# Gate logits of the first 512 tokens on VectorE, and a new order of all tasks

## The chip, the cores and the metric

The kernel runs on one core of a Trainium2 chip. Times are device microseconds (us) of one execution. Smaller is better. TensorE (PE) multiplies matrices into PSUM, VectorE (DVE), ScalarE (ACT) and GpSimd (POOL) work on tiles, and SyncE (SP) issues every DMA of this kernel.

## The reference

Two branches over 2,048 tokens with 512 features are mixed by a gate of one number per token.

```
x = A_x                                            # 2048 x 512
g = sigmoid(sum(x * gate_w, -1))                   # one gate per token
# A: attention, 32 heads of 16, causal, a window of 256 tokens
q, k, v = split_heads(x @ wqkv)
s = q @ k.T * 16 ** -0.5;  s = where(0 <= i - j < 256, s, -1e9)
a = join_heads(softmax(s) @ v) @ wo
# B: a layernorm over features, then an MLP over tokens
h = (x - mean) / sqrt(var + 1e-5)
u = gelu(h.T @ w1 + b1)                            # 512 x 1376
b = (u @ w2 + b2).T
out = g * a + (1 - g) * b
```

## The kernel before

All of x stays in SBUF (`xo`), with its transpose by blocks of 512 tokens (`XT`). The first block is transposed on PE, the other three by DMA (`xt1` to `xt3`).

The work is cut into some 1,100 named tasks, each of which runs on one engine and issues a few instructions:

- `q`, `k`, `v`: projections (chains of matmuls over 128 features each; line 670 is the helper `chain` that issues all full matmuls). `qc`, `kc`, `vc` copy their results from PSUM. The copy of the queries always runs on DVE (line 754).
- `s3.v1` and the like: scores of 128 queries of a visit (here visit 3) against 128 keys for sixteen heads, row-tiled on PE (line 942); `sj.C` are the corners of the window (line 1042); `ej...` is the exponential on ACT (line 894), `mj...` the mask, on DVE (lines 907, 974) or on POOL (line 536).
- `pv3.0` and the like: probabilities times values, column-tiled on PE (line 1087). Then `n1` to `n4` on DVE: a transpose out of PSUM (line 1178), the reciprocal of the row sums, their product with the gate's factor, and the transpose back into `xo`.
- `bs`, `ba`, `pow`, `h`: layernorm on DVE and POOL. `u0` to `u10`: the first MLP product (16 matmuls each), `ub` its bias, `gelu` in one task on ACT. `y0` to `y15`: 11 matmuls of the second MLP product and 4 of the output projection in one accumulation; `f` scales and adds the bias, `o` stores.
- The gate. For the first block (`NGP = 1`), `gate0` multiplies the transposed block with gate_w on PE (16 matmuls with one column, line 802), and `gatem0` takes the result out of PSUM. For the other blocks, `gl4` to `gl15` on DVE multiply and add up along the features (line 822), from a copy of gate_w on all partitions which the load `gw` brings. `gatee` (ACT) takes the exponential, `ez` (DVE) spreads it for `nz`.

Nothing in the kernel decides its order while it runs. `PLAN` is a written list of tasks for each engine, with the PSUM bank or buffer of each task after a colon (`s3.v1:64`). The function `arrange` (line 85) plays the lists through with costs per task, which gives the one order in which instructions are issued; each engine then works through its own list in order. The costs in `arrange` do not reach the chip, except in one respect: the order in which tasks of different engines are issued, and with it a wait that POOL gets when a two-input DVE task is near.

PE's tasks have a mode: full array (d), row-tiled scores (s), corners (c), column-tiled products (p, and h for the corners' own). The chunks of projections and MLP products may run full or column-tiled. The set `THEN` names the scores and products after which the full chunks that follow run column-tiled, that is, with four matmuls of 32 rows of output in place of one.

SP's list sets the order of loads. Before: `x0`, `wqk0` to `wqk3`, `x1.4`, the transposed load `xt1`, `wv`, `x2.8`, `bias`, `xt3`, `x3.12`, `xt2`, then w1; `gw` comes among the w1 loads. A task at the head of the list that waits holds all loads behind it. w2 lies in the memory of w1, so its loads wait for the MLP's first product.

Of the kernel before, what the change touches and what calls it, by code (L numbers as in the profile page):

```python
# [78 lines left out]
SWITCH = 0.095  # L79

BLOCK, AHEAD, FETCH, BUSY = 256, 80, 3.6, 3.0
LATENCY = {"PE": 0.22, "ACT": 0.15, "DVE": 0.12, "POOL": 0.15, "SP": 2.0}


def arrange(tasks):
# [21 lines left out]
    while len(order) < len(tasks):  # L107
# [19 lines left out]
        t.cost = t.engines[e]  # L127
        ins = t.ins
        if e == "PE":
            new = then if t.flex else t.mode  # L130
            if new != mode:
                t.cost += SWITCH
            if t.flex and new == "p":
                t.tiled = True
                ins *= 4
            if t.mode != "d":
                then = "p" if t.name in THEN else "d"
            mode = new
# [52 lines left out]
        warm:3 xta0.0.0:7 xta0.0.1:6 warmb xta0.1.1:4 xta0.1.0:5 q1_0.0:2 k3_0.0:3 k1_0.0:6 q3_0.0:1 k0_0.0:7  # L191
        q3_0.1 q0_0.0:0 k3_0.1 q1_0.1 q1_0.2 k1_0.1 k3_0.2 k0_0.1 q0_0.1 q2_0.0:5 q1_0.3 q0_0.2 q1_0.4 q0_0.3
        k3_0.3 q3_0.2 q0_0.4 k3_0.4 q3_0.3 k2_0.0:4 q2_0.1 k0_0.2 k1_0.2 k1_0.3 k0_0.3 k1_0.4 q2_0.2 q3_0.4 q2_0.3
        k0_0.4 k2_0.1 k2_0.2 k2_0.3 k2_0.4 q2_0.4 s0.v0:62 q3_1.0:0 q3_1.2 k3_1.0:1 k3_1.2 q0_1.0:7 s0.C:42 v1.0:6
        q0_1.2 s-1.C:02 v1.2 v2.0:5 v2.2 s1.v3:02 biast:4 v0.0:7 v0.2 v3.0:5 v3.2 q1_1.0:4 s1.v0:62 v5.0:1 q1_1.2
        gate0:5 v5.2 v14.0:0 s0.v1:62 v13.0:5 k2_1.0:1 v14.2 pv-1.0:6 v10.0:4 k2_1.2 v13.2 s1.v2:26 k2_2.0:0 v10.2
        v15.0:1 v12.0:5 v12.2 v15.2 k2_2.2 pv0.0:2 pv0.1 s1.v1:64 pv0.2 v4.0:1 v4.2 k3_2.0:0 k3_2.2 s2.v1:26 v7.0:5
        v7.2 k0_2.0:4 s1.C:60 k0_2.2 v6.0:3 v6.2 s2.v3:06 k0_1.0:2 k0_1.2 k1_1.0:5 k1_1.2 pv1.0:6 pv1.1 pv1.2
        s2.v0:02 v11.0:4 v11.2 v8.0:5 v8.2 pv1.3 pv1.4 s2.v2:20 q2_1.0:5 v9.0:4 q2_1.2 s2.C:26 v9.2 k1_2.0:1 k1_2.2
        u3.0:0 u3.2 s3.v1:64 u3.4 u3.6 u3.8 s3.C:26 u3.10 u3.12 u3.14 u2.0:1 s3.v2:24 pv2.0:6 pv2.1 u7.0:0 pv2.2  # L200
        pv2.3 u7.2 u2.2 s3.v0:42 u2.4 u7.4 u7.6 s3.v3:46 u7.8 u7.10 u7.12 s4.v0:62 u2.6 u2.8 u2.10 u2.12 u2.14
        s4.v1:24 pv3.0:6 pv3.1 pv3.2 pv3.3 u7.14 u10.0:1 u10.2 s5.v2:42 u10.4 u10.6 u10.8 s4.v3:62 u10.10 q0_2.0:0
        q0_2.2 s4.v2:64 u10.12 u10.14 q3_2.0:2 u0.0:3 q3_2.2 s4.C:06 u0.2 u0.4 u0.6 s6.v0:40 u0.8 u0.10 u0.12
        u6.0:2 u0.14 s5.v0:06 pv4.0:4 pv4.1 pv4.2 pv4.3 u6.2 u6.4 q2_2.0:3 s5.v1:06 u6.6 q2_2.2 u6.8 s5.C:64 u6.10
        u6.12 u5.0:3 s6.C:60 u6.14 u5.2 u5.4 s6.v2:46 u5.6 k3_3.0:2 k3_3.2 q1_2.0:1 q1_2.2 u5.8 s5.v3:46 u5.10
        u1.0:2 u1.2 s6.v1:06 u1.4 pv5.0:4 u5.12 pv5.1 pv5.2 pv5.3 s6.v3:06 u1.6 u5.14 u1.8 s7.v0:64 u1.10 pv6.0:0
        pv6.1 pv6.2 u1.12 pv6.3 s7.v1:64 u1.14 u4.0:3 u4.2 s7.v3:06 u4.4 k1_3.0:2 k1_3.2 s7.C:04 u4.6 u4.8 q0_3.0:2
        s7.v2:60 q0_3.2 u4.10 u4.12 u4.14 s8.v3:46 u9.0:2 u9.2 u9.4 s8.C:04 u8.0:3 u8.2 u8.4 u8.6 s8.v1:46 u8.8
        u9.6 u9.8 s8.v0:04 u8.10 u9.10 u9.12 u8.12 u8.14 s8.v2:06 pv7.0:4 u9.14 pv7.1 pv7.2 pv7.3 s10.v0:02
        k0_3.0:7 k0_3.2 q1_3.0:4 q1_3.2 q3_3.0:6 k2_3.0:5 k2_3.2 q3_3.2 pv8.0:0 pv8.1 pv8.2 pv8.3 y4.0:3 q2_3.0:6  # L210
        q2_3.2 y0.0:7 y0.2 y0.4 y8.0:2 y0.6 y4.2 y0.8 s9.v1:40 y4.4 y8.2 y0.10 y8.4 y0.11 y0.13 s9.v3:40 y4.6 y4.8
        y4.10 y4.11 s9.v2:60 y4.13 y8.6 y8.8 s9.C:04 y7.0:3 y8.10 y7.2 y8.11 s9.v0:60 y7.4 y8.13 y7.6 s10.C:46 y7.8
        y2.0:2 y2.2 s10.v3:06 y2.4 y7.10 y2.6 y7.11 s11.v3:46 y2.8 y7.13 pv9.0:0 pv9.1 pv9.2 pv9.3 s10.v2:64 y2.10
        y2.11 y9.0:3 y9.2 s10.v1:04 y2.13 y9.4 y9.6 s11.C:60 y9.8 y1.0:2 y1.2 s11.v2:40 y1.4 y1.6 y9.10 y1.8
        s11.v1:06 y9.11 y9.13 y1.10 y1.11 s13.v3:04 y1.13 pv10.0:6 pv10.1 pv10.2 pv10.3 s12.v2:02 y5.0:5 y10.0:4
        y10.2 s12.v0:26 y5.2 y10.4 y5.4 y10.6 s11.v0:06 y5.6 y5.8 y5.10 y5.11 s12.v1:02 y10.8 y10.10 y10.11 y5.13
        s12.v3:62 y10.13 pv11.0:0 pv11.1 pv11.2 y3.0:5 pv11.3 s13.v0:26 y3.2 y11.0:4 y11.2 s12.C:60 y3.4 y11.4
        y11.6 s13.C:62 y11.8 y11.10 y11.11 y3.6 s13.v1:20 y11.13 pv12.0:6 y3.8 pv12.1 pv12.2 pv12.3 s14.v3:20 y3.10
        y3.11 y6.0:4 y3.13 s13.v2:26 y6.2 y6.4 y12.0:5 s14.v2:06 y12.2 y12.4 y6.6 s14.v0:02 y6.8 y6.10 pv13.0:6
        pv13.1 pv13.2 y6.11 pv13.3 s14.v1:02 y12.6 y12.8 y6.13 s14.C:26 y12.10 y12.11 y12.13 y13.0:0 y14.0:1 y14.2  # L220
        y13.2 s15.A:62 pv14.0:4 pv14.1 y14.4 pv14.2 pv14.3 y13.4 s15.C:26 y14.6 y13.6 y13.8 s15.B:42 y15l.0:7 y14.8
        y15l.2 y15r.0:6 y15l.4 y15l.6 y13.10 pv15.0:4 y14.10 pv15.1 pv15.2 y15r.2 y15l.8 y15l.10 y15r.4 y13.11
        y14.11 y14.13 y13.13 y15r.6 y15r.8 y15l.11 y15l.13 y15r.10 y15r.11 y15r.13
    """,
    ACT="""
        xtc0.0.1 xtc0.1.0 xtc0.1.1 kc3_0 kc1_0 kc0_0 kc2_0 e0.v0.0:4 e0.v0.1:5 kc3_1 e0.C.1:8 e0.C.0:a e-1.C.1:7
        e-1.C.0:b vc1 vc2 e1.v3.1:2 e1.v3.0:3 vc3 e1.v0.0:6 e1.v0.1:9 vc5 gatee0 e0.v1.0:d e0.v1.1:c vc14 kc2_1
        vc13 e1.v2.1:b e1.v2.0:7 vc12 vc15 kc2_2 e1.v1.0:5 e1.v1.1:a vc4 e2.v1.1:4 e2.v1.0:8 e1.C.1:d e1.C.0:c vc7
        vc6 e2.v3.1:1 e2.v3.0:0 kc1_1 e2.v0.1:a e2.v0.0:9 vc8 vc11 e2.v2.0:b e2.v2.1:5 e2.C.1:e vc9 e2.C.0:f
        e3.v1.0:c e3.v1.1:d e3.C.0:7 e3.C.1:6 ub3 e3.v2.0:a e3.v2.1:4 e3.v0.0:b e3.v0.1:5 e3.v3.1:f e3.v3.0:e  # L230
        e4.v0.1:1 e4.v0.0:0 e4.v1.0:b e4.v1.1:4 ub7 e5.v2.1:f e5.v2.0:e e4.v3.0:a e4.v3.1:d e4.v2.0:5 ub10
        e4.v2.1:c e4.C.0:2 e4.C.1:3 e6.v0.1:9 e6.v0.0:8 gatee1 e5.v0.1:0 e5.v0.0:1 e5.v1.1:c e5.v1.0:d e5.C.0:4
        e5.C.1:5 e6.C.0:7 e6.C.1:6 e6.v2.1:a e6.v2.0:b kc3_3 e5.v3.1:g e5.v3.0:h e6.v1.0:2 e6.v1.1:3 gatee2
        e6.v3.1:g e6.v3.0:h e7.v0.0:f e7.v0.1:e ub5 e7.v1.0:g e7.v1.1:d e7.v3.0:h e7.v3.1:c e7.C.0:9 e7.C.1:8
        e7.v2.0:a e7.v2.1:b e8.v3.0:6 e8.v3.1:7 e8.C.1:3 e8.C.0:4 e8.v1.0:2 e8.v1.1:5 e8.v0.0:1 e8.v0.1:0 gatee3
        e8.v2.0:f e8.v2.1:e e10.v0.0:g e10.v0.1:h gelu e9.v1.1:b e9.v1.0:8 e9.v3.1:9 e9.v3.0:2 e9.v2.1:4 e9.v2.0:3
        e9.C.0:5 e9.C.1:i e9.v0.0:a e9.v0.1:j e10.C.1:6 e10.C.0:f e10.v3.1:0 e10.v3.0:c e11.v3.0:1 e11.v3.1:d
        e10.v2.1:7 e10.v2.0:e e10.v1.0:5 e10.v1.1:4 e11.C.1:3 e11.C.0:j e11.v2.1:b e11.v2.0:a e11.v1.0:i e11.v1.1:2
        e13.v3.0:9 e13.v3.1:8 e12.v2.1:c e12.v2.0:0 e12.v0.1:f e12.v0.0:g e11.v0.0:5 e11.v0.1:e e12.v1.1:4
        e12.v1.0:7 e12.v3.0:h e12.v3.1:e e13.v0.1:d e13.v0.0:6 e12.C.0:1 e12.C.1:j e13.C.1:3 e13.C.0:i e13.v1.0:5  # L240
        e13.v1.1:2 e14.v3.0:j e14.v3.1:b e13.v2.1:c e13.v2.0:f e14.v2.0:e e14.v2.1:a e14.v0.1:7 e14.v0.0:d
        e14.v1.1:h e14.v1.0:i e14.C.0:f e14.C.1:g f12:0 e15.A.1:c e15.A.0:h e15.C.0:j e15.C.1:5 e15.B.0:9 e15.B.1:f
        f14:1 f15l:3
    """,
    DVE="""
        const zeros bs3:1 xtc0.0.0 bs2:0 ba3 parity bs1:1 ba2 ba1 bs0:0 ba0 qc1_0 bs4:1 qc0_0 ba4 qc3_0 qc2_0 qc3_1
        bs8:1 bs9:0 qc0_1 ba8 ba9 bs11:1 biasc vc0 bs5:0 ba11 ba5 bs10:1 bs7:0 ba10 ba7 gatem0 bs14:1 qc1_1 bs6:0
        n1-1:0 ba14 h2 n2-1 ba6 ez0 vc10 nz-1:0 bs12:1 n3-1:1 ba12 bs15:0 n10:0 h11 kc3_2 ba15 n20 h4 bs13:1 nz0:1
        h5 ba13 n30:0 h8 h1 m1.C.1 kc0_1 kc0_2 h6 h3 m1.C.0 h13 h14 h9 h7 n11:2 h10 h12 h0 h15 qc2_1 gl12 n21
        m2.C.1 kc1_2 m2.C.0 m2.v1.1 gl5 gl14 m3.C.0 gl15 n12:8 gl7 m3.v0.0 n22 m3.C.1 m3.v0.1 gl13 m3.v3.0 gl6 ub2  # L250
        gl10 gl4 nz2:0 nz1:1 n13:6 gatem1 gl8 gl11 gl9 n40 n4-1 qc0_2 n31:1 n32:0 qc3_2 m4.C.0 m4.C.1 n41 ub0 ez1
        n23 n14:2 m5.v0.0 nz3:1 m6.v0.1 qc2_2 m5.v2.1 n33:1 n24 m5.v0.1 gatem2 nz4:0 ub6 m5.C.1 m5.C.0 m5.v1.0 n43
# [36 lines left out]
def kernel(  # L289
# [26 lines left out]
    EPS = 1e-5  # L316
    SCALE = DH ** -0.5
    NPE = 1
    NGP = 1
    NQ = 2  # L320
    NK = 3

# [1052 lines left out]
```

## Time and profile before

| | |
|---|---|
| median of 3 runs | 200.21 us (199.88 to 200.73) |
| profiled execution | 199.82 us, its span 198.1 us |
| PE | 193.0 us busy, 4,058 matmuls |
| ACT | 169.0 us busy |
| DVE | 156.5 us busy |
| POOL | 80.0 us busy |
| HBM read, written | 15.61 MB, 2.10 MB |
| TensorE clock granted | 1.0 of full speed |

The span runs from the first to the last instruction of the profile; the time of the execution holds 1.7 us more around it. The busy time of an engine counts overlapping instructions once, but the end of a matmul is modelled and the next one starts before it, so the distance from start to start says what a matmul costs. In the rows of a group stand the source line, the engine, the operation, outputs and inputs by name, the count, busy us, mean ns of one, and the idle time before them. An L number is a line of the kernel; a line can be that of a helper that many tasks use.

### The profile page before, as it was taken

Reading aid. Unit: us, or ns where it says so; the run is one execution under the profiler, and the core shown is the slowest. Engines: PE = TensorE matmul, PEld = TensorE weight load, DVE = VectorE, ACT = ScalarE, POOL = GpSimd, SP = SyncE. Lnnn points to the kernel's source line nnn. Section 1 sums busy time; section 2 is a strip of 40 time slices with the busy share of each in tenths; the row PEclk is TensorE's granted clock in tenths of the full one; section 3 lists DMA queues with packets and bytes.
Section 4 is the critical chain, followed back from the end, with each engine's and each line's share of the span. In section 5 each row is a group of like instructions: output and inputs, shape, how many; then the busy total and the mean of one; then the engine's idle time right before and its main releaser. Section 6 shows DMA issues by size and latency. Waiting matters only on the chain. (4 is left out here: it accounts for less than half of the span.)

```text
span 198.1 us, 9100 instructions
## 1 busy us (share of the span) xinstructions
PE 193.0 (97%) x4058; PEld 93.3 (47%) x4058; DVE 156.5 (79%) x318; ACT 169.0 (85%) x198; POOL 80.0 (40%) x118
## 2 busy tenths in 40 slices
PE   7999999999999999999999999999999999999993
PEld 3643444353635445446543554344445354554572
DVE  1799888879998988986589799636867868869683
ACT  2369999999988996998999899899899989898632
POOL 6394897525344440214223200045069335452310
PEclk9999999999999999999999999999999999999999
DMA  5999798970060000001399770000211220200002
GB/s 156 294 284 232 131 319 278 346 187 0 8 174 18 18 0 3 3 5 32 98 364 367 280 210 3 26 26 30 68 37 58 60 68 22 62 30 30 30 3 83
DMA packets 23189, 22.02 MB, mean 111 GB/s; under 512 B 7566, under 2 KB 21262, under 8 KB 23150
## 3 DMA queue, kind: packets, MB, share of 16 engines
q1 hardware_dynamic: 23150, 21.44, 36.9%
q8 instruction: 32, 0.52, 1.1%
q14 instruction: 7, 0.06, 0.1%
HBM read 15.61 MB, written 2.10 MB: 89 GB/s over the span
## 5 line engine op out<-in xcount | busy, mean ns | idle before, releaser
L894 ACT ACTIVATE et<-ps 128x1024 bf16<-128x1024 f32 (+1 forms) x94 | 89.3, 1015 | 6.1 <-PE ps L942 2.4
L536 POOL TENSOR_SCALAR_AFFINE_SELECT et<-et 128x512 bf16<-128x512 bf16 (+2 forms) x63 | 46.7, 751 | 56.0 <-ACT et L894 40.9
L894 ACT ACTIVATE XT<-ps 128x1024 bf16<-128x1024 f32 (+1 forms) x60 | 58.1, 1011 | 7.3 <-PE ps L942 4.3
L670 PEld LDWEIGHTS <-wb 128*32 128x32 bf16 (+4 forms) x645 | 32.0, 97 | 34.5 <-issue 6.5
L670 PE MATMUL pb<-ug,wb 128*32 128x512 bf16 (+4 forms) x385 | 45.5, 366 | 0.0
L670 PE MATMUL pb<-h,wb 128*128 128x512 bf16 (+2 forms) x260 | 44.5, 381 | 0.0
L536 POOL TENSOR_SCALAR_AFFINE_SELECT XT<-XT 128x512 bf16<-128x512 bf16 (+1 forms) x28 | 20.0, 720 | 46.3 <-ACT XT L894 27.4
L670 PE MATMUL pb<-XT,wqkv 128*128 128x512 bf16 (+2 forms) x190 | 32.4, 372 | 0.4 <-DMA wqkv<-in_A_wqkv_dram 0.3
L1178 DVE STREAM_TRANSPOSE et<-ps 128x1024 f32<-128x1024 f32 (+1 forms) x17 | 20.1, 1183 | 11.9 <-PE ps L1087 11.1
L1087 PEld LDWEIGHTS <-VA 128*32 128x32 bf16 (+1 forms) x1056 | 20.1, 97 | 6.6 <-issue 1.5
L942 PE MATMUL ps<-QZ,KT 32*128 32x256 bf16 (+1 forms) x496 | 23.1, 265 | 0.0
L754 DVE TENSOR_TENSOR QZ<-pb,par 128x1024 bf16<-128x1024 f32 x16 | 19.5, 1221 | 3.2 <-PE pb L670 3.2
L670 PEld LDWEIGHTS <-wqkv 128*128 128x128 bf16 (+1 forms) x190 | 12.7, 98 | 14.6 <-DMA wqkv<-in_A_wqkv_dram 0.5
L670 PE MATMUL pb<-wo,xo 128*32 128x512 bf16 (+2 forms) x152 | 18.1, 375 | 0.0
L1087 PE MATMUL ps<-et,VA 128*32 128x128 bf16 (+2 forms) x624 | 17.9, 218 | 0.0
L942 PEld LDWEIGHTS <-KT 32*128 32x128 bf16 x496 | 7.4, 92 | 20.6 <-ACT et L894 10.7
L670 PE MATMUL pb<-wqkv,XT 128*128 128x512 bf16 (+1 forms) x70 | 16.5, 381 | 0.0
L974 DVE TENSOR_TENSOR et<-et,mask 128x512 bf16<-128x512 bf16 x26 | 13.3, 510 | 2.5 <-ACT et L894 2.4
L441 DVE TENSOR_SCALAR ot<-pb,c,c 128x512 bf16<-128x512 f32 (+1 forms) x11 | 8.6, 785 | 7.4 <-PE pb L670 7.3
L1087 PE MATMUL ps<-XT,VA 128*32 128x128 bf16 (+2 forms) x432 | 13.9, 215 | 0.0
L1087 PEld LDWEIGHTS <-VZ 128*32 128x32 bf16 x832 | 13.2, 98 | 0.7
L770 DVE BATCH_NORM_STATS2 stats<-xo 128x6 f32<-128x512 bf16 x16 | 10.7, 682 | 3.1 <-DMA xo<-in_A_x_dram 3.1
(76 smaller groups left out, 199.4 us busy)
## 6 DMA issues: line engine op xcount, KB each, us to landing
wb<-in_B_w_dram SPq DMA_DIRECT2D x8, 512.0 KB, 8.2
wb<-in_B_w_dram SPq DMA_DIRECT2D x2, 2048.0 KB, 9.2
VZ<-VA SPq DMA_DIRECT2D x26, 70.0 KB, 3.0
xo<-in_A_x_dram SPq DMA_DIRECT2D x3, 512.0 KB, 5.5
out_dram<-ot SPq DMA_DIRECT2D x12, 128.0 KB, 2.4
wb<-in_B_w_dram SPq DMA_DIRECT2D x4, 352.0 KB, 5.8
wqkv<-in_A_wqkv_dram SPq DMA_DIRECT2D x4, 256.0 KB, 5.0
wb<-in_B_w_dram SPq DMA_DIRECT2D x1, 1024.0 KB, 5.3
```

The costliest lines, as they stand in the source:

```text
L441: return nc.vector.tensor_scalar(out=out_, in0=in_, scalar1=scale, scalar2=bias, op0=ALU.mult, op1=ALU.add)
L536: return nc.gpsimd.affine_select(out=out_, in_=in_, pattern=[[0, n] for n in pattern] + [[step, HB]], compare_op=op, fill=0.0, base=base_, ...
L670: made.append(nc.tensor.matmul(buf(b)[c:z_, c0:c0 + w_], lhsT=lhsT[:, c:z_], rhs=rhs, start=(j == 0), stop=(j == n - 1), skip_group_check= ...
L754: lambda k=k, b=b: nc.vector.tensor_tensor(out=QZ[:, k, :, (i % NQ) * SB:(i % NQ + 1) * SB], in0=buf(b)[:, None, :].to_broadcast([P, 2, SB ...
L770: f"bs{t_}", {"DVE": 0.67}, lambda b=b, t_=t_: nc.vector.bn_stats(buf(b)[:], xo[:, t_, :]),
L894: lambda e=e, b=b, shape=shape: nc.scalar.activation(out=shape(buf(e)), in_=shape(buf(b)), func=ACT.Exp, scale=SCALE),
L942: made.append(nc.tensor.matmul(to[:, :, done:done + m], lhsT=keys(j if x == "A" else j - 1, k)[rows], rhs=q[rows], start=True, stop=True, ...
L974: made.append(nc.vector.tensor_tensor(out=v, in0=v, in1=m.to_broadcast(list(v.shape)), op=ALU.mult))
L1087: return lambda: nc.tensor.matmul(to(), lhsT=v() if callable(v) else v, rhs=buf(e)[rows, col:col + n], start=first, stop=last, tile_positi ...
L1178: lambda: nc.vector.transpose(out=view(buf(tr).bitcast(FP32)), in_=view(buf(o))), [last], takes=[tr], uses=[o],
```

## The change

The gate of the first block moves to DVE: `NGP` becomes 0, so that the tasks `gate0` (PE) and the PSUM form of `gatem0` are gone and `gl0` to `gl3` are new on DVE, with `gatem0` in its SBUF form. In SP's list `gw` moves ahead of `wv`, and both ahead of `x1.4`; `xt3` and `bias` come before `x2.8`, and `vs13` moves from the middle of the stores to the w1 loads.

`arrange` gets other costs: `TURN`, a cost for each pair of PE modes in place of the one `SWITCH`; `cost_of`, which corrects costs by engine and kind; other latencies; 3.1 us for a block of instructions in place of 3.6, and 3.5 us in place of 3.0 on top while a large load runs. The task `gelu` is counted at 7.0 us in place of 8.3.

All five lists and the set `THEN` are new. On POOL 35 masks go to DVE and 19 come back. ACT takes two more copies of K, three more bias additions and one more output, and gives three copies of V to DVE. On PE, where the order of nearly everything moves, the first part and one later part are shown.

```diff
-SWITCH = 0.095
-
-BLOCK, AHEAD, FETCH, BUSY = 256, 80, 3.6, 3.0
-LATENCY = {"PE": 0.22, "ACT": 0.15, "DVE": 0.12, "POOL": 0.15, "SP": 2.0}
+TURN = {
+    "d": dict(d=0, s=0.100, p=0.100, c=0.098, h=0.100),
+    "s": dict(d=0.116, s=0, p=0.115, c=0.105, h=0.114),
...
+BLOCK, AHEAD, FETCH, BUSY = 256, 80, 3.1, 3.5
+LATENCY = {"PE": 0.21, "ACT": 0.15, "DVE": 0.11, "POOL": 0.12, "SP": 2.0}
+
+
+def cost_of(t, e):
+    c, n = t.engines[e], t.name
+    if e == "PE":
+        return c - 0.02 if t.mode == "s" else c * 0.738 if t.mode == "c" else c
+    if e == "DVE":
+        return max(0.1, c - 0.06)
+    if e == "ACT":
+        return c - 0.085 if n[:2] in ("vc", "kc", "ub") else c - 0.008 if n[0] == "e" else c
+    if e == "POOL" and n[0] == "m" and ".C" in n:
+        return c * 1.14
+    return c
...
-        t.cost = t.engines[e]
+        t.cost = cost_of(t, e)
...
-            if new != mode:
-                t.cost += SWITCH
+            t.cost += TURN[mode][new]
             if t.flex and new == "p":
                 t.tiled = True
                 ins *= 4
+                t.cost += 0.0025 * t.ins
...
     PE="""
-        warm:3 xta0.0.0:7 xta0.0.1:6 warmb xta0.1.1:4 xta0.1.0:5 q1_0.0:2 k3_0.0:3 k1_0.0:6 q3_0.0:1 k0_0.0:7
...
+        warm:5 xta0.0.1:4 warmb xta0.0.0:7 xta0.1.1:6 xta0.1.0:5 k1_0.0:2 k0_0.0:1 q3_0.0:7 q3_0.1 k0_0.1
...
+        v15.0:0 v15.2 v6.0:1 v6.2 pv1.0:6 pv1.1 pv1.2 pv1.3 pv1.4 s2.v0:24 v9.0:0 v9.2 q2_1.0:1 s2.v2:26
...
+        s8.v1:46 u9.4 u9.6 u9.8 s8.v0:62 u8.8 u8.10 u9.10 s8.v2:24 u9.12 pv7.0:6 u8.12 u8.14 pv7.1 pv7.2
+        u9.14 q1_3.0:0 s10.v0:24 q1_3.2 q2_3.0:1 pv7.3 pv8.0:2 pv8.1 pv8.2 pv8.3 q2_3.2 q3_3.0:4 k0_3.0:6
...
     DVE="""
-        const zeros bs3:1 xtc0.0.0 bs2:0 ba3 parity bs1:1 ba2 ba1 bs0:0 ba0 qc1_0 bs4:1 qc0_0 ba4 qc3_0 qc2_0 qc3_1
...
+        zeros bs0:0 const bs1:1 ba0 xtc0.1.0 ba1 bs2:0 parity ba2 bs3:1 ba3 qc3_0 qc1_0 gl1 qc0_0 bs5:1 h0
+        qc2_0 gl3 gl0 bs6:0 vc5 gl2 ba5 ba6 bs7:1 gatem0 bs4:0 ba4 qc3_1 ba7 qc1_1 bs8:1 vc12 biasc ba8
...
     SP="""
-        x0.0 x0.2 wqk0 wqk1 wqk2 wqk3 x1.4 xt1 wv x2.8 bias xt3 x3.12 xt2 vs0 w1_02 w1_03 vs1 w1_22 vs2 gw w1_12
...
+        x0.0 x0.2 wqk0 wqk1 wqk2 wqk3 gw wv x1.4 xt1 xt3 bias x2.8 vs0 xt2 x3.12 vs1 w1_03 w1_12 w1_01 w1_02
+        vs2 vs13 w1_00 w1_11 vz2:1 w1_23 vz6:0 w1_13 w1_10 vz5:2 vz3:1 w1_20 w1_21 w1_22 vz4:1 vz14:1 wo
...
-    NGP = 1
+    NGP = 0
...
-    gelu = add("gelu", {"ACT": 8.3}, emit_gelu, ub)
+    gelu = add("gelu", {"ACT": 7.0}, emit_gelu, ub)
```

## The prediction

> **What bounds the kernel now.** I read the page first: who is busy, and how the busy share runs over the 40 slices.
>
> ```profile
> span 198.1 us, 9100 instructions
> ...
> PE 193.0 (97%) x4058; PEld 93.3 (47%) x4058; DVE 156.5 (79%) x318; ACT 169.0 (85%) x198; POOL 80.0 (40%) x118
> ...
> PE   7999999999999999999999999999999999999993
> ...
> q8 instruction: 32, 0.52, 1.1%
> ```
>
> PE is full from the second slice to the last but one, but a busy PE need not be PE at its peak, so the waits come next. This is everything that PE's matmuls waited for:
>
> ```profile
> PE pb L591 <- DVE ug L518: 1.4, 1, 1.4
> PE pb L670 <- DMA wqkv<-in_A_wqkv_dram: 0.3, 1, 0.3
> PE pb L670 <- ACT XT L894: 0.2, 1, 0.2
> ```
>
> Two of the three lie before 6.6 us. Then the spacing inside PE's work, in the chain that ended last (start, length, what):
>
> ```profile
> 151.56 0.33 PE ps L942 x8
> 151.89 1.41 PE pb L670 x24
> 153.29 0.33 PE ps L942 x8
> 153.63 1.83 PE pb L670 x8
> 155.46 0.33 PE ps L942 x8
> 155.79 1.62 PE pb L670 x7
> ```
>
> Eight full matmuls of 512 columns take 1.83 us, seven take 1.62: 0.21 for one more (0.216 between two starts in the timeline), and 0.105 us left in each stretch. So PE streams without a hole, and each change between full matmuls, row-tiled scores and column-tiled products costs about 0.1 us. [...]
>
> To see how much hole there is at all, I split PE's 4,058 matmuls by the names in PE's list and took, for each task, the time from its first matmul to the next task's first. Tasks of one kind with the same successor have one value to within 0.01 us (two full 512-column matmuls: 0.432 before their own kind, 0.525 to 0.539 before another). The sum of these medians is 191.56 us; what all tasks take over their medians is 1.25 us: 0.46 waiting for the first weights at 6.1 us, 0.16 from two slow matmuls there, and about 0.6 net in the body (0.25 at the scores s10.v0 at 113 us, 0.13 at y9.6 at 143 us, the rest under 0.1 each). ACT and DVE come closest behind: from start to start, ACT's list holds 161.3 us of work and DVE's 145.8.
>
> **The change, part by part.**
>
> Gate off PE. Two rows of the groups, shapes kept apart (busy us, mean ns, idle before):
>
> ```profile
> L822 DVE SCALAR_TENSOR_TENSOR junk<-xo,gwr 128x512 bf16<-128x512 bf16 x12 | 8.3, 695 | 0.1
> ...
> L802 PE MATMUL pb<-gwc,XT 128*128 128x1 bf16 x16 | 0.5, 163 | 0.0
> ```
>
> The 16 one-column matmuls hold PE for 0.404 us (start of the gate to the next start, 23.02 to 23.43) between full matmuls, with no mode change: -0.40 us on the path. In their place DVE gets four more instructions of the first row, 0.62 each from start to start: +2.5 us on DVE, within the first 17 us.
>
> New PE order. Walking both lists with the set THEN, PE changes mode 169 times before and 165 times after; 74 of the chunks that may be tiled ran column-tiled, 68 do now. A tiled chunk takes the same 0.432 us, so this frees no time; it takes 33 matmuls and as many weight loads off the instruction stream, and with the gate's 16 leaves 4,009 matmuls. Four changes at 0.105 are -0.42 us. Summing the medians over the new list, kind by kind, gives 190.71: -0.85 us, of which the gate is 0.40 and the order 0.45. Four tasks have no row; I took them from their neighbours (0.315 for one 512-column matmul before another mode, 0.558 for a product before corners); 0.1 us either way.
>
> DVE and ACT. DVE takes 35 masks from POOL and gives back 19, takes 3 copies of V, gives 2 of K, 3 bias additions and one output. With the durations above, DVE's list grows from 145.8 to 152.0 us and ACT's from 161.3 to 163.4, of about 190. In total both are hidden by PE. Where it is tight is the stretch up to the projections' end. Summing DVE's list up to the transpose n1 of visit 1, DVE has 37.5 us of list time before and 38.2 after, and PE reaches that point by 43.0 before and 40.2 after: the spare falls from 5.5 to 2.0 us. Of this, 2.05 us goes at once, since DVE's first query copy cannot start before its projection ends at 9.65. Adding the lists from 25.85 us on (PE's end of visit -1), n1 of visit 1 would start at 41.1 by work, 41.0 by PE. In the trace of before, DVE loses about 0.9 us between the same two points to pauses that are no wait for PE (0.45 after the corner mask at 38 us, 0.2 each at 27.4 and 33.9). So I expect it about 0.5 us late, 0 to 1.2. The score task s2.v2 reuses that PSUM pair 0.15 us after the copy would free it: PE waits about 0.4 us there. What hid it before were other chunks: s2.C, the next user, came with DVE waiting 1.05 us for PE at 42.6 us.
>
> PSUM reuse elsewhere. For each task on PE I took the previous user of its bank, its copy or exponential (1.02, 1.25 or 0.6 us) and the handovers (0.25 and 0.07): before, the tightest are -0.38, -0.07 and -0.02 us, after -0.09, -0.09, -0.03 and -0.02. The new order is as tightly packed, not worse: about 0.2 less waiting.
>
> Loads. SP's list now has the gate weights and V's weights before x1.4 and both transposes in a row. The queue before:
>
> ```profile
> 3.75 0.43 SPq L454 DMA_DIRECT2D xo<-in_A_x_dram  x1
> 4.23 5.73 SPq L463 DMA_TRANSPOSE XT<-in_A_x_dram  x1
> 10.01 0.57 SPq L475 DMA_DIRECT2D wqkv<-in_A_wqkv_dram  x1
> ```
>
> 1 MB of query and key weights came in from 4.4 to 8.4 us, 0.26 MB per us; the 0.64 MB put ahead costs 2.5 us. x1.4 then lands at about 12.6 instead of 10.1, the first transpose at 14.5 instead of 12.0, the second near 17.5, the biases by 21.5. First uses by the new lists: 13.7 (statistics on DVE), 15.8 (v5.0), 19.1 (v14.0), 22.1 (biast). Cover of 0.5 to 1.6 us each: no cost, and one us of PE per us if it is gone. V's weights land near 10.9, before v1.0 at 12.4. The first key and query matmul still waits for wqk0, which moves past nothing. vs13, now ahead of most w1 loads, holds SP until V's tile 13 is copied at about 35.6; w1_00 is then in by 41 and used at 46.0.
>
> Instruction blocks. [...] The trace shows PE's 32 blocks (q8, 16,384 bytes each): counted at 80 to 100 instructions ahead of each block's end, a fetch starts about 1.0 us later in quiet stretches and 2.6 to 4.4 us later beside the w1 and w2 loads, and takes 1.0 to 1.5 us. The shortest stretch between two block ends was 3.5 us before and is 3.1 after (pv14 to pv15), which a quiet 2.3 us covers. But pv7 to pv8, at 110.3 to 113.6, has 3.4 us while w2 is being loaded, where it had 5.1. Bounds: 0 (a delay of 1.8, as at 113.9 before) to 2.2 us (4.4 + 1.2 - 3.4); I take 0.
>
> The end. PE's last matmul to the end of the span is unchanged: the left half's output moves to DVE, but its 0.55 us is over before the right half's matmuls are. The last transposes need 2.53 us after pv15.2 and PE has 2.50 us of other work: 0.
>
> Sum: -0.85 on PE's list; the body's old waits (0.6) give way to about as many new ones (0.4 at s2.v2, some tenths elsewhere). The profiled execution took 199.82 us for its span of 198.1, so 198.97 for one of 197.25; the runs' median, 200.21, is 0.39 higher: 199.4 us.
>
> **The rivals.**
> - The waits go as well: the new order leaves almost no hole, and the body's 0.6 goes too: -1.4, 198.8 us. For it: the bank sums. Against it: DVE's lost spare.
> - The floor is lower but PE runs in step with ACT, which has 2.1 us more work and waited only 1.1 us between 20 and 40 us: the gain is waited away: 200.2. What speaks against it is that ACT's list up to the scores of 108 us still leaves 10 us of spare.
> - Slower by DVE: n1 of visit 1 and the masks behind it come late by the whole 2.0 us that DVE lost between 20 and 40 us, not 0.5, and the next transposes inherit it: +2.0 less 0.85, 201.4. It decides once DVE's lateness passes 0.85 + 0.15 = 1.0 us.
> - Slower by an instruction block: at pv8, +2.2 less 0.85: 201.6. It decides at a block that is ready over 4.25 us after the block end at pv7.
>
> **How the numbers follow.** Forecast 0.42, waits gone 0.20, in step with ACT 0.15, DVE 0.14, block 0.09. A measurement of this kernel cannot tell less than 0.5%, 1.0 us, from no change. The forecast's own range is 198.9 to 199.9; a third of it lies below 199.2, so faster is 0.20 + 0.14 = 0.34. Slower is the two last cases, less a small stall that the floor pays for: 0.21. The rest, 0.45, is the same. The range leaves out a tenth at each end: 198.2 (waits gone and 0.6 of startup) to 201.5.
>
> **What would show it.** Right: no L802 matmuls, 4,009 matmuls, PE's busy time near 192; 16 rows of L822, four before 20 us; the 0.105 us stretches unchanged. A wait of PE at L942 near 42 us behind the transpose L1178 confirms DVE's late start. A hole on PE at 113.6 beside a block fetch is the last rival; holes at 14 to 20 us say that the loads came late. A span of 197 or less would mean I overrated the waits.

## The result, and the profile after

| | before | after |
|---|---|---|
| median | 199.99 us (199.44 to 201.06, 20 runs) | 201.59 us (200.80 to 203.30, 20 runs) |
| profiled execution, its span | 199.82, 198.1 us | 201.18, 199.5 us |
| PE's first matmul, last end | 1.38, 195.00 us | 1.25, 196.12 us |

The ratio is 1.0077, interval 1.0059 to 1.0096: 1.6 us slower, where 0.8 us faster was forecast. The profiled execution of after is one of its faster ones, 0.4 us under its median. From its page, as for before:

```profile
span 199.5 us, 8994 instructions
...
PE 192.9 (97%) x4009; PEld 92.4 (46%) x4009; DVE 158.0 (79%) x339; ACT 170.4 (85%) x201; POOL 64.0 (32%) x101
...
PE   7799999999999999999999989999999999999993
...
q8 instruction: 31, 0.51, 1.0%
```

4,009 matmuls and 16 gate instructions on DVE, four of them before 20 us, are as forecast. PE's busy time, forecast near 192, is 192.9, and one slice of PE in the middle falls to 8. All that PE's matmuls waited for:

```profile
PE pb L616 <- DVE ug L543: 1.3, 1, 1.3
PE pb L695 <- DMA wqkv<-in_A_wqkv_dram: 1.0, 1, 1.0
PE ps L1112 <- issue: 0.8, 1, 0.8
```

The third is new. "Issue" means that the trace shows nothing PE waited for. The spacing within PE's work, in the chain that ended last, is the old one: seven matmuls together with the change of mode take 1.62 us, scores 0.33.

```profile
164.46 1.41 PE pb L695 x24
165.87 0.36 PE ps L1067 x32
166.23 1.62 PE pb L695 x7
167.85 0.33 PE ps L967 x8
```

Split by tasks as in the prediction, PE's list sums to 190.71 us by the medians of before: -0.84, as worked out. But the tasks take 4.16 us over these medians where they took 2.07 (the prediction's 1.25 is too low: from PE's first matmul at 1.38 to its last end at 195.00 are 193.62 us, and 191.56 from that leaves 2.06). With 0.13 us of earlier start and a tail behind PE's last matmul that grew by 0.24, this gives the 1.4 us between the spans. Where the excess is in after:

| PE's task | at us | over the median | what stood before it |
|---|---|---|---|
| last transpose of x, first keys and queries | 5.4 | 0.86 (before 0.62) | first weights |
| pv0.0, pv0.1 | 30.2 | 0.31 | the last of POOL's masks |
| s5.v1 | 77.4 | 0.36 | issue |
| u9.12 | 110.0 | 0.16 | not explained; 0.15 to 0.16 in every profile of this order |
| pv8.1 | 115.4 | 0.95 | issue |
| pv15.1 | 191.6 | 0.24 | issue |

The largest, in PE's timeline (start, length, what, and the idle time before it): in the midst of one task, on tiles that were in use already.

```profile
115.37 0.19 PE L1112 MATMUL ps<-et,VZ 128*32 128x64 bf16 x1
116.33 0.24 PE L1112 MATMUL ps<-et,VZ 128*32 128x64 bf16 x7 [0.77 <-issue]
```

The hole at s5.v1 shows in the weight loads:

```profile
77.28 0.12 PEld L967 LDWEIGHTS <-KT 32*128 32x128 bf16 x7 [0.42 <-ACT XT L919]
77.76 0.09 PEld L967 LDWEIGHTS <-KT 32*128 32x128 bf16 x1 [0.36 <-issue]
```

The three holes with "issue" stand, to within one or two, at PE's instructions 2,497, 4,289 and 7,873, counting matmuls, weight loads and PE's own waits: 63 short of the 10th, 17th and 31st multiple of 256. q8 moved one packet of 16,384 bytes, an instruction block, for about every 256 of these instructions: 31 for 8,055 in after, 32 for 8,157 in before. Each hole ends 1.31 to 1.40 us after such a packet has landed. And the tail: `f15l` on DVE waits for a store to free its buffer, and the last output behind it starts 0.25 us late.

```profile
194.46 0.45 DVE L1238 STREAM_TRANSPOSE xo<-zt 128x256 bf16<-128x256 bf16 x1
195.88 1.08 DVE L466 TENSOR_SCALAR ot<-pb,c,c 128x256 bf16<-128x256 f32 x2 [0.97 <-DMA out_dram<-ot]
```

### The profile page after: what moved, and what is told of

Its sections match the earlier page's. It is cut to its first block, busy times and chain, and to the rows that moved or that the text cites. A ratio compares the mean times of both kernels' runs of the same rounds, so it can differ in the third digit from the quotient of the medians.

```text
span 199.5 us, 8994 instructions
## 1 busy us (share of the span) xinstructions
PE 192.9 (97%) x4009; PEld 92.4 (46%) x4009; DVE 158.0 (79%) x339; ACT 170.4 (85%) x201; POOL 64.0 (32%) x101
## 4 chain that ended last, share of the span: by engine, by line
PE 85%; POOL 5%; DMA 4%; ACT 2%; issue 2%; DVE 1%; SPq 0%; DVEq 0%
PE pb L695 63%; PE ps L1112 10%; PE ps L967 9%; POOL et L561 4%; PE ps L1067 3%; DMA wqkv<-in_A_wqkv_dram 2%; DMA out_dram<-ot 2%; ACT et L919 1%; DVE ot L466 1%; POOL rstd L806 1%; SPq L479 0%; ACT ot L463 0%; PE ps L1023 0%; ACT KT L627 0%; POOL rstd L805 0%
## 5 line engine op out<-in xcount | busy, mean ns | idle before, releaser
L919 ACT ACTIVATE et<-ps 128x1024 bf16<-128x1024 f32 (+1 forms) x103 | 97.8, 1015 | 6.2 <-PE ps L967 3.2
L561 POOL TENSOR_SCALAR_AFFINE_SELECT et<-et 128x512 bf16<-128x512 bf16 (+2 forms) x60 | 41.7, 702 | 96.5 <-ACT et L919 57.8
L919 ACT ACTIVATE XT<-ps 128x1024 bf16<-128x1024 f32 (+1 forms) x51 | 49.4, 1014 | 3.7 <-PE ps L967 0.8
L695 PEld LDWEIGHTS <-wb 128*32 128x32 bf16 (+3 forms) x660 | 32.1, 97 | 35.4 <-issue 6.9
L695 PE MATMUL pb<-ug,wb 128*32 128x512 bf16 (+5 forms) x334 | 44.8, 368 | 0.0
L695 PE MATMUL pb<-h,wb 128*32 128x512 bf16 (+2 forms) x326 | 44.7, 381 | 0.0
L1203 DVE STREAM_TRANSPOSE et<-ps 128x1024 f32<-128x1024 f32 x14 | 17.5, 1249 | 11.8 <-PE ps L1112 11.8
L561 POOL TENSOR_SCALAR_AFFINE_SELECT XT<-XT 128x512 bf16<-128x512 bf16 (+1 forms) x14 | 9.5, 678 | 26.7 <-ACT XT L919 18.3
L695 PE MATMUL pb<-wqkv,XT 128*128 128x512 bf16 x64 | 16.7, 381 | 0.0
L932 DVE TENSOR_TENSOR XT<-XT,mask 128x1024 bf16<-128x1024 bf16 (+1 forms) x16 | 10.6, 665 | 4.8 <-ACT XT L919 4.6
```

What stands on the lines that cost most here:

```text
L561: return nc.gpsimd.affine_select(out=out_, in_=in_, pattern=[[0, n] for n in pattern] + [[step, HB]], compare_op=op, fill=0.0, base=base_, ...
L695: made.append(nc.tensor.matmul(buf(b)[c:z_, c0:c0 + w_], lhsT=lhsT[:, c:z_], rhs=rhs, start=(j == 0), stop=(j == n - 1), skip_group_check= ...
L919: lambda e=e, b=b, shape=shape: nc.scalar.activation(out=shape(buf(e)), in_=shape(buf(b)), func=ACT.Exp, scale=SCALE),
L932: return nc.vector.tensor_tensor(out=v, in0=v, in1=m[:, None, :].to_broadcast([P, n, w]), op=ALU.mult)
L1203: lambda: nc.vector.transpose(out=view(buf(tr).bitcast(FP32)), in_=view(buf(o))), [last], takes=[tr], uses=[o],
```

## The experiments

Theory A: the loss is above all stalls on instruction blocks. It counts from the place where the holes stand, 63 instructions before a block's edge; PE's coming to it is called the crossing. By the theory a block is fetched from there on (0.86 us after the crossing ahead of the hole at s5.v1, 2.03 at pv8.1, 1.12 at pv15.1), and PE stands still if it runs through 256 more instructions before that block is usable; at s5.v1 this was 3.26 us after the crossing (74.50 to 77.76). What starts a fetch is not in the trace: the 31 blocks of after began to move from 0.7 us ahead of the crossing to 3.2 behind it, so that it is the crossing is my estimate. Against it: holes of another kind (data, masks, loads), or the gate itself on DVE. Times are medians; the kernel before, measured beside them, had 200.06 to 200.26.

### Block boundaries moved in the old order

```diff
-    add("warm", ..., lambda: warming(5, 512), ...)
+    add("warm", ..., lambda: warming(4, 512) + warming(33, 64), ...)
```

> Edit: the kernel before, with 32 narrow warm-up matmuls (64 columns, 64 instructions with their weight loads) more in the first 4 us, where PE has nothing to do until the first tokens arrive. No list, no task and no transfer changes; only the place of PE's block boundaries in its program moves by 64 instructions. Theory A [...]: counted from the trace of before, nine stretches become shorter than 3.25 us (near 60, 75, 93, 116, 150, 168, 177 and 188 us), and the kernel takes 6 to 10 us longer, about 207 to 210 us, with holes of 0.5 to 2 us on PE at those places and no work added behind the start. Rival B (blocks are fetched in time whatever their place, the holes of the changed kernel are something else): within 0.5 us of before.

Measured: 207.81 us, one run, +7.6. What PE's matmuls waited for:

```profile
PE pb L670 <- issue: 3.7, 5, 1.0
PE ps L1087 <- issue: 2.5, 2, 1.7
PE pb L591 <- DVE ug L518: 1.4, 1, 1.4
```

Seven holes, at 96, 102, 120, 156, 176, 186 and 198 us, 7.9 us over the medians together. Each ends 1.24 to 1.53 us after a block landed. Behind the start no task, list or transfer is changed. That block edges alone can stall PE is shown by this run. The count of places was not exact: 60 and 75 us did not stall, and 102 us was not on the list.

### The load beside pv8.1

SP's list, w2 later:

```diff
-    w2_0 w2_1 vz8:0 w2_2 o0 vz9:2 o7
+    w2_0 vz8:0 vz9:2 w2_1 w2_2 o0 o7
```

> Edit: the changed kernel, SP's list alone: the loads w2_1 and w2_2 go behind vz9, so that their 1.4 MB move after 114 us instead of from 111 to 116. Nothing on PE, DVE, ACT or POOL changes. Theory A (the hole of 0.95 us at pv8.1 is an instruction block that came late [...] beside the w2 load): the fetch starts near 113 us, the hole at pv8.1 shrinks from 0.95 to 0.2 us or less, and the kernel gains 0.6 to 1.0 us on the changed one. Rival B (pv8.1 waited for data, or for something else on PE): the hole stays where it is, 0 gained. Rival C (w2 is needed sooner than I think): the hole goes and a wait of PE for the load comes at y0.4 or y0.8 near 120 us, as long or longer.

Measured: 207.46 us, ratio 1.0382 (1.0350 to 1.0413). The hole at pv8.1 is gone, and a wait for w2 near 120 us is far longer than I had reckoned: I had moved 3.4 MB, not 1.4, since w2_1 alone is 2 MB, and vz9 could go only at 115.2 us. Behind that wait the granted clock fell for a while (5 and 8 tenths in the page's two slices from 123 to 134 us, 0.98 over these runs; 1.0 in after), so the time is not the wait alone.

```profile
PE pb L695 <- DMA wb<-in_B_w_dram: 5.5, 1, 5.5
PE pb L616 <- DVE ug L543: 1.3, 1, 1.3
```

The stretches of one us show why the hole went (in order: length, busy share and count of PE, PEld, DVE, ACT, POOL, then clock, DMA share, GB/s). After:

```profile
112.00:113.00 1.00, 1.00 (x64) 0.66 (x52) 1.00 (x2) 1.00 (x2) 0.00 (x0) 1.00 1.01 401
113.00:114.00 1.00, 1.00 (x18) 0.33 (x11) 1.00 (x4) 0.88 (x3) 0.00 (x0) 1.00 0.95 389
114.00:115.00 1.00, 1.00 (x44) 0.47 (x45) 0.87 (x2) 1.00 (x2) 0.00 (x0) 1.00 1.01 213
115.00:116.00 1.00, 0.56 (x52) 0.41 (x37) 0.62 (x1) 0.98 (x2) 0.67 (x1) 1.00 0.62 205
```

With w2 later:

```profile
112.00:113.00 1.00, 1.00 (x56) 0.56 (x44) 1.00 (x2) 1.00 (x3) 0.00 (x0) 1.00 0.09 16
113.00:114.00 1.00, 1.00 (x18) 0.33 (x11) 1.00 (x4) 0.88 (x2) 0.00 (x0) 1.00 0.00 0
114.00:115.00 1.00, 1.00 (x51) 0.57 (x53) 0.77 (x2) 1.00 (x2) 0.01 (x1) 1.00 0.00 0
115.00:116.00 1.00, 1.00 (x106) 1.00 (x93) 0.71 (x1) 0.98 (x2) 0.66 (x1) 1.00 0.00 0
```

The DMA queues are empty but for the block itself. The queues by packets, MB and share, in after from 112 to 114 us, where q8 has no packet, and from 114 to 115 us:

```profile
q1 hardware_dynamic: 201, 0.78, 96.9%
...
q8 instruction: 1, 0.02, 6.2%
```

All that moved from 112 to 114 us with w2 later:

```profile
q8 instruction: 1, 0.02, 4.3%
```

There the fetch began 0.45 us after the crossing at 111.9 us; in after it was 2.03 us, at 114.01, when the 1 MB of w2 beside it had all but ended. PE's work up to there is nearly the same.

A first try to hold only this load failed: I took it for w2_1, which in fact goes out at 103 us. What goes out at 109.7 is the first part of w2_2.

```diff
+    held["w2_1"].deps.append(held["pv7.2"])
+            if t.name == "w2_1":
+                tc.add_manual_dep(first, seen.name, ...)
```

> Edit: the changed kernel; the load w2_1 waits on SP until PE has done pv7.2 (near 112.6 us) instead of starting at 109.7, and vz8 goes ahead of it. PE's list and THEN are untouched. In the run with w2 behind vz9 [...] pv8.1 had no hole, but w2 came 5.7 us too late. Theory A (a fetch beside a large load starts late): the same here, hole at pv8.1 gone, w2_1 lands near 117.5 to 118, ahead of y0.4 at 119.6, so the gain on the changed kernel stays: -0.8 to -1.0 us, about 200.6 us. Rival (the load only moves the wait): a wait for w2 at y0.4 or y0.8 of 0.5 us or more.

Measured: 201.71 us, 1.0099 (1.0059 to 1.0139). w2_1 still went out at 103.0 us, the hole was 1.0 us, and the run tells nothing more. The right one, in `w2_2`:

```diff
+            if hi == full_:
+                nc.sync.dma_start(w2[:F - full_ * P, full_, :], ...)
             nc.sync.dma_start(w2[:, lo:hi, :], ...)
-            if hi == full_:
-                nc.sync.dma_start(w2[:F - full_ * P, full_, :], ...)
```

> Edit: the changed kernel; in the task w2_2 the two DMAs change places, so that the small one (0.4 MB, which has to wait for PE until 113.0 us) holds the large one (1 MB) back from 109.7 to 113.4 us. Nothing else differs; PE's, DVE's and ACT's programs are the same. (The kernel with w2_1 held did not do what its edit says: its loads went out at 110.0 us as before, and its block fetch began at 114.3 us, again when the 1 MB load ended.) Theory A: between 111 and 114 us no large load runs, [...] the hole at pv8.1 (0.95 to 1.15 us in all runs of this order with that load beside it) is 0.2 us or less: -0.8 to -1.0 us, about 200.7 us. Rival: w2_2 lands too late for y0.8 near 121 us and PE waits there instead.

Measured: 202.37 us, 1.0112 (1.0061 to 1.0162): no gain. In the profile pv8.1 is down to 0.2 us over its median, but the load now ran from 114 to 120 us, the next fetch began only at 119.6, and PE stood for 0.8 us near 122 (the row's 0.61 counts from the modelled end of the matmul before):

```profile
122.05 1.45 PE L695 MATMUL pb<-ug,wb 128*128 128x512 bf16 x6 [0.61 <-issue]
```

It ends 1.49 us after that block landed. So neither side was right: the load did move the wait, but onto the next block, not onto its own data.

### The gate by itself

In the old order:

```diff
-    NGP = 1
+    NGP = 0
-    DVE ... ba10 ba7 gatem0 bs14:1      PE ... q1_1.2 gate0:5 v5.2
+    DVE ... ba10 ba7 gl0 gl1 gl2 gl3 gatem0 bs14:1      PE ... q1_1.2 v5.2
-    SP ... wv x2.8 ... vs2 gw w1_12
+    SP ... wv gw x2.8 ... vs2 w1_12
```

> Edit: the kernel before with the gate alone moved: gate0 off PE's list, gl0 to gl3 on DVE ahead of gatem0, gw behind wv on SP. All other places in the lists, costs and THEN as before. PE's program is 32 instructions shorter from 23 us on. The prediction's first step says -0.40 us. Theory A adds that the block boundaries move by 32 instructions: stretches near 88 and 183 us fall to 2.4 us and cost about 0.85 us each, so the sum is +1.0 to +1.6 us, slower than before. Rival (blocks do not matter): -0.4 us. Rival (DVE is late by its 2.5 us more): PE waits for DVE between 24 and 45 us.

With 32 instructions more in PE's idle start:

> Edit: as in the kernel with the gate alone moved, and 16 narrow warm-up matmuls (32 instructions) more in PE's idle first 4 us, so that from 23 us on every block boundary stands where it stood in the kernel before. Theory A: the stalls of the gate alone go, and what is left is the gate itself, -0.4 us (-0.2 to -0.6). Rival (blocks do not matter): the same time as the gate alone. Rival (DVE late): slower than before by what DVE lost between 24 and 45 us.

Measured: 205.12 us, 1.0253 (1.0227 to 1.0279), and 203.36 us, 1.0163 (1.0128 to 1.0198). The 1.8 us between them are the moved boundaries: holes of 1.55 us at 97 us and 0.1 to 0.2 at three further places, in the first only; and not at the two places counted beforehand. The stretches meant there lie at 91 and 188 us, PE being 3 and 5 us late by then, and are 2.5 and 2.4 us long; they cost 0.2 us and nothing. Their fetches began early, 0.3 us after the crossing as I count it and 0.9 ahead of it, so a short stretch alone does not decide. The rest is the DVE rival. With the boundaries kept:

```profile
PE ps L1090 <- POOL et L539: 1.8, 1, 1.8
PE pb L673 <- DVE QZ L757: 1.5, 2, 1.4
```

A bank waits for a copy of queries, and pv-1 for a mask that POOL, itself behind DVE's statistics, has not done. In the old lists, at the place tried, there is no room for the gate on DVE.

In the new lists, the gate put back on PE:

```diff
-    NGP = 0
+    NGP = 1
-    PE ... v4.2 pv-1.0:4        ACT ... vc2 gatee0 ... vc4 e0.v1.0
+    PE ... v4.2 gate0:7 pv-1.0:4     ACT ... vc2 ... vc4 gatee0 e0.v1.0
-    DVE gl0 gl1 gl2 gl3, ... bs7:1 gatem0 ... bs11:0 bs9:1
+    DVE ... bs7:1 ... bs11:0 gatem0 bs9:1
-    THEN ... s3.v1
```

A first version had `gatem0` behind n1-1 and `gatee0` behind e0.v1.1:

> Edit: the changed kernel with the gate of the first block back on PE: NGP = 1, gate0 behind v4.2 on PE, gl0 to gl3 off DVE, gatem0 behind n1-1 on DVE and gatee0 behind e0.v1.1 on ACT. s3.v1 leaves THEN, which takes 36 instructions off PE's program at 46 us against gate0's 32, so that the block boundaries behind stand 4 instructions from where they stood. The prediction's first step expects +0.40 us on the changed kernel, 202.0 us. Rival (DVE's 2.5 us more cost the changed kernel as much as PE gains, as they cost the kernel before): equal to the changed kernel or faster, 201.2 to 201.6 us, with fewer waits of PE for DVE before 45 us.

It took 203.22 us, 1.0161 (1.0130 to 1.0192), since the scores s0.v1 need bank 7, which the gate held until its late readout: 1.2 us of waiting that I had put in myself. The version above has the readout early:

> Edit: the changed kernel with the gate of the first block back on PE: gate0 behind v4.2, its readout gatem0 on DVE behind bs11 (ahead of the transpose n1-1, so that bank 7 is free for s0.v1), gatee0 behind vc4 on ACT, gl0 to gl3 off DVE, s3.v1 out of THEN so that the block boundaries behind 46 us stand 4 instructions from where they stood. The prediction's first step: +0.40 us on the changed kernel, all of it on PE's list at gate0. If DVE's 2.5 us were not hidden in the new order, part of the 0.4 comes back as fewer waits of PE before 45 us, and the time is equal.

The changed kernel beside it:

> The changed kernel once more, unedited, beside the others of this call. All theories: 201.2 to 201.9 us, holes of 0.9 to 1.1 us at pv8.1 and 0.36 us at s5.v1 again, at the same instructions.

Measured: 202.06 us (201.47 to 202.63) with the gate on PE, 202.32 us (201.24 to 203.04) without, six runs each. The +0.40 did not come; with this scatter the runs leave open a few tenths either way. On PE the gate takes 0.47 us again, so the 0.40 is on PE's list. But the two kernels do not differ by the gate alone: in the profile with the gate on PE the hole at s5.v1 is absent, and the wait for POOL's mask at pv0.0 too (0.64 and 0.26 in the unedited kernel's profile beside it). Whether the 0.40 reaches the end stays open. The unedited kernel's profile, its slowest run (203.04 us), shows the same holes, wider: 0.64 at s5.v1, 1.28 at pv8.1, 0.27 at pv15.1, and two that the first profile had at 0.08 and 0: 0.90 us at u7.0 (50 us), 0.44 at u10 (65 us). So part of what the new order loses comes and goes between executions. Its ratio to before was 1.0077 first and 1.0115 (1.0084 to 1.0145) here, so a few tenths of a us between kernels measured at different times prove nothing.

### The mends

The small ones, without and with the failed hold of w2_1:

```diff
-    THEN ... s5.v0 ... pv14.3
+    THEN ... s5.C s15.A
-    POOL ... m1.v0.0 m0.v1.0 m0.v1.1 m0.v0.1
+    POOL ... m0.v1.0 m0.v1.1 m0.v0.1 m1.v0.0
-    SP ... o13 o11 o12 o14      DVE ... f15l:1 f15r:0
+    SP ... o11 o12 o13 o14      DVE ... f15l:0 f15r:2
```

> Edit: the changed kernel with three small mends and the hole at pv8.1 left in. THEN loses s5.v0 and pv14.3 and gets s5.C and s15.A (the same number of column-tiled chunks by 47 us later, but fewer instructions in the stretches at 74.5 and 188.4 us). On POOL the mask m1.v0.0 goes behind m0.v0.1, which pv0.0 waits for. On SP o11 and o12 go ahead of o13, and f15l takes buffer 0 and f15r buffer 2, so that the last output no longer waits for the store of f13. Theory A expects -0.36 at s5.v1, -0.24 at pv15.1, -0.27 at pv0.0 and -0.25 at the end: -1.1 us on the changed kernel, about 200.5 us (-0.7 to -1.3). Rival (the time lies in the order as such, the holes are replaced by others): within 0.4 us of the changed kernel.

> Edit: both sets of mends together on the changed kernel. If the holes found in the trace account for the loss, and nothing new comes in their place, -2.0 us on the changed kernel: 199.6 us, -0.2% against before (199.2 to 199.9). If the new order is worse than before for another reason: 200.5 us or more.

Measured: 200.90 us, 1.0048 (1.0028 to 1.0068), and 201.17 us, 1.0048 (1.0029 to 1.0068). In the profile of the first the holes at s5.v1, pv15.1, pv0.0 and in the tail went (the exchange in THEN took eight chunks out behind pv14.3 and put three in, which costs 0.2 us of mode changes). But:

```profile
PE ps L1112 <- issue: 0.7, 1, 0.7
PE pb L695 <- DMA wb<-in_B_w_dram: 0.6, 1, 0.6
```

The second is u7.0 at 50 us, which waits for the last loads of w1: 0.74 and 0.49 us over its median. PE, 0.3 us ahead since 30 us, runs into a load that does not move with it. (In the unedited kernel's second profile the 0.90 us at u7.0 are put down to DVE, but there too the last packets of w1 came at 50.4 us.) SP's timeline in the first of the two kernels shows what held it:

```profile
27.88 0.69 SPq L744 DMA_DIRECT2D VS<-VA  x1
35.72 0.46 SPq L743 DMA_DIRECT2D VS<-VA  x1
```

Between the two SP stands before `vs13`, with eight w1 loads behind it. With the mask mended and that moved:

```diff
-    SP ... vs2 vs13 w1_00 ... w1_22 vz4:1
+    SP ... vs2 w1_00 ... w1_22 vs13 vz4:1
```

> Edit: the changed kernel; on POOL the mask m1.v0.0 goes behind m0.v0.1, and on SP vs13, which keeps SP waiting from 28.3 to 36.0 us for a tile of V, goes behind w1_22, so that the w1 loads no longer wait for it. In the runs with the mask mended alone, the 0.31 us won at pv0.0 (30 us) came back as 0.5 to 0.7 us of waiting for w1_10 at u7.0 (50 us). Theory B (PE at 50 us runs against a load that vs13 holds back, so a gain ahead of 50 us cannot pass): with both mended the 0.31 at 30 us and the 0.08 at 50 us go and nothing waits at 50 us: -0.4 us on the changed kernel, about 201.2 us. If another wait takes its place: no change.

Measured: 201.35 us, 1.0047 (1.0029 to 1.0065), 22 runs. Neither the wait at 30 us nor one at 50 us is left (u7.0 0.07), so theory B holds for the waits. Its 0.4 us cannot be read from the time: 201.35 lies within the scatter named above, and pv8.1 waits 1.3 us in this profile. All of it together:

```diff
 w2_2's DMAs swapped; mask, vs13, f15l and f15r as above
-    THEN pv3.3 pv7.2 s11.C s12.v2 s3.v1 s3.v2 s5.v0 s8.v3
+    THEN pv2.3 s0.v1 s10.v0 s11.v1 s15.A s5.C s6.v0 s8.v0 s9.v2
```

> Edit: the changed kernel with everything: w2_2's DMAs swapped, the mask and vs13 moved, f15l and f15r on buffers whose stores are over, and eight names of THEN replaced by nine others, chosen so that no stretch of 256 instructions of PE is shorter than 3.35 us as the trace's durations give it. From the holes: -0.95 (pv8.1) -0.6 (s5.v1, pv15.1) -0.4 (pv0.0, u7.0) -0.25 (end), so -2.2 us on the changed kernel: 199.4 us, 0.3 to 0.5% under before. If the mends only move the waits: 200.2 us or more.

The same with THEN changed by s5.v0 and s5.C alone:

> Edit: as the kernel with everything, but in THEN only s5.v0 gives way to s5.C, so the tight stretches at 62, 111 and 183 to 191 us stay at 3.05 to 3.45 us. Theory A: 0.3 to 0.8 us slower than the kernel with everything, in holes at block boundaries near 65, 188 and 191 us; 199.7 to 200.2 us. If stretches just above 3 us are no matter: equal to it.

Measured: 200.09 us, 1.0004 (0.9981 to 1.0028), and 200.05 us, 1.0006 (0.9980 to 1.0031). The loss is gone, the forecast gain does not appear, and the loosened THEN makes no difference. What was left at 122 us was again a block whose fetch began only when the swapped load had all but ended (1.46 us in the profile of the first, no such hole in the second, where the load ended at 118 us). So the load in three parts:

```diff
-            nc.sync.dma_start(w2[:, lo:hi, :], ...)
+            nc.sync.dma_start(w2[:, lo, :], ...)
             nc.sync.dma_start(w2[:F - full_ * P, full_, :], ...)
+            nc.sync.dma_start(w2[:, lo + 1, :], ...)
```

> Edit: all small mends (s5.v0 for s5.C in THEN, mask, vs13, buffers of the last outputs), and w2_2 in three DMAs: the first 0.5 MB at 109.7 us as soon as it may, then 0.4 MB and 0.5 MB at 113 us. So the 0.5 MB is over near 112.3 us, [...] and the other 0.9 MB is over by 117.5 us, before the next block is needed near 120 us. Theory A: no hole over 0.3 us at pv8.1 nor at 122 us; 199.3 to 199.8 us, 0.1 to 0.4% under before. Rival (a load beside PE's dense stretch costs time in any cut): 200 us or more, with a hole at one of the two places.

With `gw` behind x1.4 as well, and with the loosened THEN instead:

> Edit: as with w2 split, and the gate's weights gw go behind x1.4 on SP instead of ahead of wv. If the early gw slows the last of the query and key weights, the first 14 us get 0.2 to 0.4 us shorter (the waits of PE before 8 us fall), 199.1 to 199.6 us. If not (the waits there vary from execution to execution anyway), equal to the kernel with w2 split.

> Edit: as with w2 split, and the exchange of names in THEN of the kernel with everything (eight out, nine in), by which no stretch of 256 instructions of PE is shorter than 3.35 us by the trace's durations. If the remaining holes at 65 and 191 us are block stalls, they go: -0.5 us on the kernel with w2 split, 199.6 us. If waits for ACT and DVE take their place: 200.1 us, equal.

Measured: 200.10 us, 1.0005 (0.9989 to 1.0021); 200.35 us, 1.0014 (0.9998 to 1.0030), so the place of `gw` does not matter; 200.03 us, 1.0008 (0.9992 to 1.0024); 22 runs each. Both holes around the load are gone (0.3 us or less), and no version beats before. The profile of the first still stalls for 0.47 us at 64 us and 0.50 at pv15.1, each ending 1.6 us after a block landed; in the other two these are 0.3 us or less. The waits of PE with the loosened THEN:

```profile
PE pb L695 <- issue: 4.1, 26, 0.2
PE pb L616 <- DVE ug L543: 1.3, 1, 1.3
PE pb L695 <- DMA wqkv<-in_A_wqkv_dram: 1.1, 1, 1.1
PE ps L967 <- ACT XT L919: 0.3, 1, 0.3
PE pb L695 <- DVE XT L999: 0.2, 1, 0.2
PE pb L695 <- ACT ug L1278: 0.2, 1, 0.2
```

The first line is single matmuls whose record is missing from this trace (its page has 3,996 matmuls to 4,030 weight loads, where after has 4,009 of each); they are no holes. No block stall over 0.3 us is left, yet the tasks take 3.23 us over the medians, where before had 2.07: 0.4 at s9.v1, which waits for ACT now that PE is early, 0.3 around 120 us, 0.16 at u9.12, the rest in the first 14 us and in tenths. By this one profile, that is where the gain of the shorter list goes.

## Why the prediction was wrong

- Gate off PE and the new order, -0.85: the size on PE's list is right (-0.84 in the trace). That it reaches the end is not shown: the gate put back cost nothing that could be measured, in a kernel that also lost two holes, and with the large holes mended the time is that of before.
- "I take 0" for the instruction blocks is the step that failed. 0.95 us at pv8.1, 0.36 at s5.v1 and 0.24 at pv15.1 make 1.55 us, of the 2.2 us between the 198.97 forecast for the profiled execution and its 201.18. Two errors. "A quiet 2.3 us covers" left out the time from a block's landing to its first use, 1.31 to 1.40 us here: from crossing to first use the two quiet blocks took 3.3 and 3.4 us, and the three stretches have 2.9 to 3.4 us without their holes. And I checked two stretches alone, the one at pv7 and one that I took for the shortest, 3.1 us where before had 3.5. Counted where the holes stand, the shortest is 2.9 us at s5.v1, and before has 3.0 at 169 us. The rival was placed right: it was to decide at 4.25 us, the block took 4.35, and its end time of 201.6 is the measured one, but by luck: its price was 0.95, not 2.2, and other losses made up the rest. Its chance of 0.09 was too low for bounds whose lower end I took from a single fetch.
- "The body's old waits give way to about as many new ones" failed: 0.31 us for the mask at pv0.0 came new (POOL's list was not summed, though it lost masks and kept the last one that pv0 needs), and with the holes mended, waits for ACT and w1. The old waits were also more than the 0.6 us I had: 2.06 less the 0.62 at the start leaves 1.4.
- "Loads: no cost" holds for the first 30 us. I followed `vs13` to w1_00, used at 46 us, but not to w1_10 behind it, used at 50: 0.08 us in one profile, 0.9 in the other.
- "The end: 0" failed by 0.25: I asked when DVE is free, not when the buffer of `f15l` is.
- DVE late at s2.v2: no such wait. n1 of visit 1 started at 41.41 us, 0.3 after PE was through with that visit at 41.09; but I had PE there by 40.2, so PE's own 0.9 us of delay hid what DVE may have lost, and the 0.5 is not tested. Of the pauses that I called no wait for PE, the one at 38 us is one: the copy of K at 39.02 came 0.2 us after its product ended at 38.82. The rival of DVE did not decide in this order, and was right for the gate alone in the old one.

## What to carry to other kernels

PE, 97% busy, had a second list here that no task shows: its own instructions in blocks of 256, whose edges alone cost 7.6 us when they moved by 64 instructions (one run). Before packing an engine closer, count the time from edge to edge (2.9 us without its hole at s5.v1 was too short here), and keep large loads away from the short stretches (beside 1 MB the fetch began 2.03 us after the crossing, without it 0.45). And a gain in the middle passes to the end only if every load, mask and buffer behind it has as much spare (here 0.3 us won at 30 us came back as 0.5 to 0.7 at 50); sum these before the gain is booked.

## What the hardware showed that I had not expected

- In 36 places of 14 profiles where a block stalled PE, it was used 1.24 to 1.69 us after it had landed and had taken 0.9 to 1.5 us to move; in the 19 with quiet DMA queues it had begun to move 0.7 to 1.6 us after the crossing. 64 instructions more, ahead of all work, cost 7.6 us in one run.
- Beside a load of 1 MB the fetch began when that load ended or all but ended: at 114.01 us in after (2.03 us after the crossing) and at 119.6 us with w2_2 swapped (3.9 us), against 0.45 us after the crossing without a load.
- The holes stand 63 instructions before the block's edge, to within two (2,497, 4,289 and 7,873 in after). Why 63, no run shows.
